# Scaled products kept in PSUM, and two small loads and scalings moved, in a windowed attention with a Sinkhorn-gated mixture of experts

## The chip, the cores and the metric

The kernel runs on one core of a Trainium2 chip: TensorE (PE; PEld is its weight load), VectorE (DVE), ScalarE (ACT), GpSimd (POOL), and SyncE (SP), which here issues all transfers. TensorE writes into PSUM, of which the kernel uses eight banks; GpSimd's operands all lie in SBUF. The metric is the time of one execution in device microseconds. The kernel before takes 1623.35 us, the median of three runs (1622.08 to 1623.9).

## What is computed

The reference, cut to what matters:

```python
scores = scale * q @ k.T, masked to 0 <= i - j < 64      # q, k, v: (4, 8, 576, 64)
x = softmax(scores) @ v                                  # as (2304, 512)
P = exp(x @ w_gate - max); 8 times: P /= rows, P /= columns, P *= N / E
for e in range(8):
    h = np.maximum(x @ w1[e], 0.0)                       # w1: (8, 512, 1024)
    out += P[:, e:e + 1] * (h @ w2[e])                   # w2: (8, 1024, 512)
```

Everything is float32. The kernel gets it from a faster matmul format by splitting each operand into a high part (rounded) and a low part (what is left), and adding three products: high x high, high x low, low x high.

## The kernel before

Attention and gate come first, up to about 200 us, together with the first half of expert 0 for all rows; for the rows of the later passes that half's output is stored in DRAM (`yd`). Then the 2304 rows go in three passes of 768 (six tiles of 128) through the remaining 7.5 experts.

The *first pass* (200 to 668 us) works in 15 units of two groups, a group being 256 hidden columns. It also prepares the weights, and stores them split in DRAM (`w1d`, `w2d`).

*Passes two and three* (668 to 1140, 1140 to 1620 us) work with blocks. A block `First` (F) makes a group of the first layer, a block `Second` (S) half of a unit's second layer. Each does a 2 x 2 block product in seven instead of eight multiplications, which are its steps 1, 5, 6, 2, 7, 3, 4, each a *product* of six matmuls with 384 columns. Its results build up in three PSUM banks: `a` gets products 1 and 2; `b` starts as a copy of `a`, gets 6, 7 and 4; `c` gets 5 and 3. In the trace they are qa, qb and qc. Each has two buffers, six banks in all, and the tag `y` takes the other two. A bank that the next product adds to must first have been read by whoever needs its present value.

In an F block (line 1005) VectorE makes from them what the second layer multiplies: relu(x) times the row's probability, in one operation (`scaled`, line 988, which reads the probabilities, spread over the partitions, from `pb`). The four results are r22 from `a` (after step 2), c22 from `b` plus a copy (step 7), cr from `c` (step 3), and sm0 from `b` (step 4); sums of these (sm0 to sm3) make slots 3 to 6 of the operand `G`, and r22, c22, cr make slots 2, 0 and 1. ScalarE writes the high part of a slot (`hi`, line 992), VectorE or GpSimd the low part (`lo`, line 996, on GpSimd for slot 2 and, in `part_s`, for the sums). The adds of an F block's step 4 (sm1, sm3 and the low part of slot 1) are put off until after step 6 of the next block (`late_sums`).

In an S block each product is added by VectorE to the output in `acc` (line 1105); the next product into that bank waits for it.

The order is written out by hand. A unit of a pass is two F blocks and the two S blocks of the unit before, in one sequence, where steps 1 and 5 of a block stand inside the block before. Each engine does its instructions in program order, and other work is hung on steps by `hook`: weight splits (ScalarE high, GpSimd low, from the buffers `wr`), loads of `w1c`, of `pb`, and between passes the new rows x (`new_x`, `high`, `low`) and the finish of the pass before: transposes (`turn`), the scaled half expert's rows (`load_y`, `scale_y`), their sum (`finish`) and the store.

## Time and profile before

| | |
|---|---|
| runs | 1623.35 us median (1622.08 to 1623.9) |
| profiled execution | 1622.74 us, of which the span is 1620.6 |
| PE busy | 1566.8 us (97%), 9665 matmuls |
| DVE busy | 1063.5 us (66%), 1745 instructions |
| ACT busy | 754.2 us (47%), 1619 |
| POOL busy | 1090.2 us (67%), 973 |
| chain that ended last | PE 69%, DVE 22%, issue 4%, ACT 2%, DMA 2% |

A row of the timeline has its start, its duration, engine, line, operation and operands, and in brackets the idle time before it with what ended that. Matmuls overlap, so the busy time of PE is no sum of work: the distance from one start to the next says what a product costs. The lines are those of the kernel before.

### The profile page before, as it was taken

What the parts mean: (1) busy time and instruction counts of PE and PEld (TensorE: products, weight loads), DVE (VectorE), ACT (ScalarE), POOL (GpSimd) and SP (SyncE); (2) the same over time, 40 slices, a digit from 0 to 9 for tenths busy, and PEclk for the clock granted to TensorE, in tenths of its full rate; (3) what the DMA queues carried; (4) which work ended last, traced back from release to release, by engine and by line L of the source; (5) the groups of instructions that cost most, each with busy time, mean ns of one, the idle gap of its engine ahead of it and who ended that gap; (6) DMA issues with size and microseconds to landing.
All of it is one profiled execution on the core that took longest, in us unless ns stands there. A gap on an engine that the chain in (4) does not pass through costs nothing.

```text
span 1620.6 us, 26692 instructions
## 1 busy us (share of the span) xinstructions
PE 1566.8 (97%) x9665; PEld 1476.6 (91%) x9665; DVE 1063.5 (66%) x1745; ACT 754.2 (47%) x1619; POOL 1090.2 (67%) x973
## 2 busy tenths in 40 slices
PE   8999999999999999899999999999799999999998
PEld 7888899899899889799999999999799999999998
DVE  7666466665455555567667667767666776676676
ACT  6666545434434434354444444445454444444443
POOL 6245476768767865277767777777777677677674
PEclk9999999999999999899999999999999999999999
DMA  9876476676767566865556555556755565565553
GB/s 222 199 174 151 126 277 235 228 253 221 269 213 258 214 224 242 286 199 198 191 172 198 190 178 187 194 185 228 245 196 175 170 211 181 167 209 184 163 188 104
DMA packets 226513, 328.32 MB, mean 203 GB/s; under 512 B 69922, under 2 KB 149390, under 8 KB 222414
## 3 DMA queue, kind: packets, MB, share of 16 engines
q1 hardware_dynamic: 226382, 326.63, 62.3%
q8 instruction: 76, 1.25, 0.3%
q14 instruction: 55, 0.45, 0.1%
HBM read 232.67 MB, written 86.96 MB: 197 GB/s over the span
## 4 chain that ended last, share of the span: by engine, by line
PE 69%; DVE 22%; issue 4%; ACT 2%; DMA 2%; POOL 0%; SPq 0%; DVEq 0%
PE yp L275 14%; PE qb L216 12%; PE qa L216 10%; PE qc L216 9%; PE qb L1097 8%; DVE sm L1003 8%; DVE G L996 4%; PE hp L561 3%; PE yp L575 3%; PE qc L1097 3%; DVE acc L1105 3%; PE qa L1097 3%; DVE sm L988 2%; DVE qc L1003 1%; DVE cr L988 1%
## 5 line engine op out<-in xcount | busy, mean ns | idle before, releaser
L216 PE MATMUL qb<-xc,w1c 128*128 128x384 f32 x1620 | 324.7, 338 | 13.6 <-DVE c L1003 7.7
L216 PEld LDWEIGHTS qb<-xc,w1c 128*128 128x128 f32 x1620 | 287.1, 189 | 15.6 <-DVE c L1003 8.4
L996 POOL TENSOR_TENSOR G<-sm,G 128x384 fp32r<-128x384 f32 x176 | 202.1, 1149 | 132.8 <-ACT G L992 132.8
L275 PE MATMUL yp<-w2c,g 128*128 128x512 f32 x1080 | 251.3, 391 | 0.5 <-DVE acc L294 0.5
L275 PEld LDWEIGHTS yp<-w2c,g 128*128 128x128 f32 x1080 | 201.7, 188 | 42.8 <-DVE acc L294 1.2
L216 PE MATMUL qa<-xc,w1c 128*128 128x384 f32 x1080 | 214.9, 338 | 0.0
L216 PE MATMUL qc<-xc,w1c 128*128 128x384 f32 x1080 | 213.0, 336 | 0.0
L216 PEld LDWEIGHTS qa<-xc,w1c 128*128 128x128 f32 x1080 | 192.3, 189 | 1.2
L216 PEld LDWEIGHTS qc<-xc,w1c 128*128 128x128 f32 x1080 | 190.1, 188 | 0.0
L1105 DVE TENSOR_TENSOR acc<-qb,acc 128x384 f32<-128x384 f32 x171 | 94.6, 553 | 122.1 <-PE qb L1097 116.5
L726 POOL TENSOR_TENSOR wp<-wr,wp 128x512 fp32r<-128x512 f32 x104 | 134.0, 1300 | 49.2 <-ACT wp L725 44.5
L177 POOL TENSOR_TENSOR w2c<-stg,w2c 128x512 fp32r<-128x512 f32 x60 | 84.5, 1429 | 108.9 <-PE qb L216 96.2
L996 POOL TENSOR_TENSOR G<-r,G 128x384 fp32r<-128x384 f32 x120 | 131.5, 1106 | 38.3 <-ACT G L992 38.2
L726 POOL TENSOR_TENSOR w2c<-wr,w2c 128x512 fp32r<-128x512 f32 x102 | 132.0, 1305 | 35.0 <-ACT w2c L725 29.1
L992 ACT CAST G<-sm 128x384 fp32r<-128x384 f32 x180 | 92.0, 511 | 99.1 <-DVE sm L1003 99.1
L1097 PE MATMUL qb<-G,w2c 128*128 128x384 f32 x552 | 114.6, 342 | 12.5 <-DVE acc L1105 12.5
L992 ACT CAST G<-r 128x384 fp32r<-128x384 f32 x120 | 61.3, 511 | 130.8 <-DVE r L988 84.0
L1097 PE MATMUL qb<-G,wp 128*128 128x384 f32 x528 | 108.8, 341 | 11.3 <-DVE acc L1105 10.7
L1097 PEld LDWEIGHTS qb<-G,w2c 128*128 128x128 f32 x552 | 96.1, 188 | 21.8 <-DVE acc L1105 21.8
L1097 PEld LDWEIGHTS qb<-G,wp 128*128 128x128 f32 x528 | 92.2, 188 | 18.9 <-DVE acc L1105 18.0
L294 DVE SCALAR_TENSOR_TENSOR acc<-yp,prob,acc 128x512 f32<-128x512 f32 x72 | 53.9, 749 | 68.5 <-PE yp L275 67.9
L457 POOL TENSOR_TENSOR s<-s,rr 128x512 f32<-128x512 f32 x36 | 37.5, 1040 | 79.3 <-DVE rr L456 71.8
(186 smaller groups left out, 2993.7 us busy)
## 6 DMA issues: line engine op xcount, KB each, us to landing
w1c<-w1d SPq DMA_DIRECT2D x120, 512.0 KB, 6.4
w1d<-w1c SPq DMA_DIRECT2D x30, 1792.0 KB, 7.5
w1c<-w1d SPq DMA_DIRECT2D x180, 256.0 KB, 3.1
stg<-in_moe_w_dram SPq DMA_DIRECT2D x66, 512.0 KB, 4.2
wr<-w2d SPq DMA_DIRECT2D x118, 256.0 KB, 3.2
wr<-in_moe_w_dram SPq DMA_DIRECT2D x88, 256.0 KB, 2.8
w2d<-tf SPq DMA_DIRECT2D x30, 512.0 KB, 4.9
pb<-prow SPq DMA_DIRECT2D x32, 192.0 KB, 7.0
```

The lines of the kernel that those rows point to most:

```text
L177: nc.gpsimd.tensor_tensor(out=w[:, 1], in0=src[:, j], in1=f32(w[:, 0]), op=ALU.subtract)
L216: nc.tensor.matmul(bank, lhsT=w[:, ws, a, kk, :], rhs=xc[xs][:, b, kk, :], start=(first and j == 0), stop=(j == 5), skip_group_check=not f ...
L275: nc.tensor.matmul(yp, lhsT=g[:, a, o:o + P], rhs=w[:, x, :], start=(i == 0), stop=(i == 11))
L294: nc.vector.scalar_tensor_tensor(out=at, in0=yp, scalar=pr, in1=at, op0=ALU.mult, op1=ALU.add)
L561: nc.tensor.matmul(hp, lhsT=w1s[c][:, a, kk, :], rhs=xs[j][:, b, kk, :], start=(i == 0), stop=(i == 3 * KD - 1))
L575: nc.tensor.matmul(yp, lhsT=g[:, a, o * P:(o + 1) * P], rhs=w[:, x, :], start=(i == 0), stop=(i == 11))
L726: nc.gpsimd.tensor_tensor(out=t[:, :, 1, :], in0=r, in1=f32(t[:, :, 0, :]), op=ALU.subtract)
L992: nc.scalar.copy(out=self.g[:, k, 0, :], in_=src)
L996: eng.tensor_tensor(out=self.g[:, k, 1, :], in0=src, in1=f32(self.g[:, k, 0, :]), op=ALU.subtract)
L1003: eng.tensor_tensor(out=dst, in0=x, in1=y, op=op)
L1097: nc.tensor.matmul(bank, lhsT=W[p, u, wp][:, g, y, cols], rhs=G7[p, 2 * u + g][:, gp, x, :], start=(start and j == 0), stop=(j == 5), skip ...
L1105: nc.vector.tensor_tensor(out=at, in0=src, in1=at, op=ALU.add)
```

## The change

The Relu'd and scaled products of an F block are written back into their banks instead of into tiles r22, c22, cr and sm0 in SBUF; c22 gets one of the two `y` banks for itself, and the transposes the other. r22, which GpSimd still reads, becomes a copy made by ScalarE. The low part of slot 2 moves to VectorE. `pb` gets one fixed buffer for even experts (`pb_a`) and one for odd ones, and the first is loaded within the first pass. The x rows for the next passes' sums take a tile of the ring `tf`. The six stored rows of the half expert are scaled in VectorE's last add (`finish`) and no longer by ScalarE; two of them have buffers of their own and are loaded earlier, and the splits of x stand a step earlier.

The diff, cut to its core:

```diff
+    pb_a = lambda: big.tile([P, 2, TP // 2, P], F32, tag="pb_a", name="pb_a")
+    PB = {}
...
-        ps["y"] = lambda: ps_m.tile([P, 512], F32, tag="y", name="yp2")
+        n_y = [0]
+
+        def y_bank(i):
+            return ps_m.tile([P, 512], F32, tag=f"y{i}", name=f"y{i}", bufs=1)
+
+        def next_y():
+            n_y[0] += 1
+            return y_bank(n_y[0] % 2)
+
+        ps["y"] = next_y
+
+        def load_pb(p, e, t):
+            PB[p, e] = t
+            rows = prow[p].rearrange("(o n e) c -> e n o c", n=2, e=E + 1)[e]
+            for n in range(2):
+                nc.sync.dma_start(out=t[:, n], in_=rows[n].partition_broadcast(P))
...
-                x = ring_b.tile([P, KD, 2 * P], F32, tag="xr2", name="xr2")
+                x = r_tf.new()
...
                 if last:
+                    load_pb(1, 0, pb_a())
                     load_w1(0)
...
-            def load_pb(p, e):
-                t = PB[p, e] = new("pb", [P, 2, TP // 2, P], F32, 2)
-                rows = prow[p].rearrange("(o n e) c -> e n o c", n=2, e=E + 1)[e]
-                for n in range(2):
-                    nc.sync.dma_start(out=t[:, n], in_=rows[n].partition_broadcast(P))
+            def next_pb(p, e):
+                load_pb(p, e, new("pb", [P, 2, TP // 2, P], F32, 1) if e % 2 else pb_a())
...
                         G.product(2, self.a, False)
-                        self.scaled(self.r22, self.a, 0)
-                        self.hi(2, self.r22)
+                        self.scaled(self.a, self.a, 0)
+                        nc.scalar.copy(out=self.r22, in_=self.a)
+                        self.hi(2, self.a)
                     elif n == 7:
-                        self.c22 = new("c22", [P, NB], F32, 1)
+                        self.c22 = y_bank(0)[:, :NB]
                         G.product(7, self.b, False)
                         self.add(self.c22, self.b, self.p5)
                         self.scaled(self.c22, self.c22, 1)
                         self.hi(0, self.c22)
-                        self.lo(2, self.r22, nc.gpsimd)
+                        self.lo(2, self.a)
                     elif n == 3:
-                        self.cr = new("cr", [P, NB], F32, 1)
                         G.product(3, self.c, False)
                         self.add(self.c, self.c, self.u2)
-                        self.scaled(self.cr, self.c, 1)
-                        self.hi(1, self.cr)
+                        self.scaled(self.c, self.c, 1)
+                        self.hi(1, self.c)
                         self.lo(0, self.c22)
...
-                        self.scaled(sm[0], self.b, 0)
-                        self.add(sm[0], sm[0], self.r22)
+                        self.scaled(self.b, self.b, 0)
+                        self.add(sm[0], self.b, self.r22)
...
                             self.add(sm[1], self.c22, sm[0], ALU.subtract)
-                            self.add(sm[3], self.cr, sm[1])
+                            self.add(sm[3], self.c, sm[1])
                             self.add(sm[2], sm[1], self.r22, ALU.add, nc.gpsimd)
-                            self.lo(1, self.cr)
+                            self.lo(1, self.c)
...
-            def load_y(p, ts):
+            def load_y(p, ts, own=False):
                 for t in ts:
-                    ys[t] = side["x"][:, ORDER[t]].rearrange("p k c -> p (k c)")[:, 0:DM]
+                    ys[t] = new("ys", [P, DM], F32, 2) if own else side["x"][:, ORDER[t - 2]].rearrange("p k c -> p (k c)")[:, 0:DM]
...
-            def scale_y(p, t):
-                nc.scalar.activation(out=ys[t], in_=ys[t], func=AF.Copy, scale=prob[:, FIRST[p] + t, 0:1])
...
-                    yps[t] = ps_m.tile([P, 512], F32, tag=bank if bank == "y" else f"q{bank}", name="yt")
+                    yps[t] = y_bank(bank) if bank in (0, 1) else ps_m.tile([P, 512], F32, tag=f"q{bank}", name="yt")
...
-                nc.vector.tensor_tensor(out=ys[t][:, cols], in0=yps[t][:, cols], in1=ys[t][:, cols], op=ALU.add)
+                nc.vector.scalar_tensor_tensor(
+                    out=ys[t][:, cols], in0=ys[t][:, cols], scalar=prob[:, FIRST[p] + t, 0:1], in1=yps[t][:, cols], op0=ALU.mult, op1=ALU.add)
...
+            next_pb(1, 1)
             out_rows(0, range(TP))
-            for e in range(2):
-                load_pb(1, e)
...
-                    for k, (blk, st) in zip(ORDER[:5], ((a, 6), (b, 5), (b, 6), (a, 7), (a, 3))):
+                    for k, (blk, st) in zip(ORDER[:5], ((a, 5), (a, 6), (b, 5), (b, 6), (a, 7))):
                         hook(blk, st, lambda k=k: (high(k), low(k, nc.gpsimd)))
-                    for k, st in zip(ORDER[5:], (7, 3)):
-                        hook(b, st, lambda k=k: high(k))
-                        hook(b, 4, lambda k=k: low(k, nc.vector))
-                    hook(b, 3, lambda p=p: load_y(p, range(3)))
-                    hook(b, 4, lambda p=p: load_y(p, range(3, 6)))
+                    for k, (blk, st) in zip(ORDER[5:], ((a, 3), (b, 7))):
+                        hook(blk, st, lambda k=k: (high(k), low(k, nc.vector)))
+                    hook(a, 2, lambda p=p: load_y(p, range(2), True))
+                    hook(b, 3, lambda p=p: load_y(p, range(2, TP)))
                     nf = plans[p][1]
-                    for t, (blk, st) in enumerate(((nf[0], 3), (nf[0], 4), (nf[1], 6), (nf[1], 2), (nf[1], 7), (nf[1], 3))):
-                        prior.setdefault((blk, st), []).append(lambda p=p, t=t: (scale_y(p, t), turn_all(p, t)))
+                    for t, (blk, st) in enumerate(((nf[0], 2), (nf[0], 3), (nf[1], 6), (nf[1], 2), (nf[1], 7), (nf[1], 3))):
+                        prior.setdefault((blk, st), []).append(lambda p=p, t=t: turn_all(p, t))
```

The rows that follow show where instructions stand on an engine, in program order: line, operation, result and operands, columns. Lines of the changed kernel are its own.

VectorE, from step 7 of a unit's second F block on into the S block, before (G_10826 is the operand, c_0_10847 is c22, L1105 are S's adds):

```order
L1003 TENSOR_TENSOR c_0_10847<-qb,p_0_10785 128x384
L988 SCALAR_TENSOR_TENSOR c_0_10847<-c_0_10847,pb_10269 128x384
L1003 TENSOR_TENSOR qc<-qc,u_0_10812 128x384
L988 SCALAR_TENSOR_TENSOR cr_10858<-qc,pb_10269 128x384
L996 TENSOR_TENSOR G_10826<-c_0_10847,G_10826 128x384
L1105 TENSOR_TENSOR acc<-qc,acc 128x384
L988 SCALAR_TENSOR_TENSOR sm_0_10885<-qb,pb_10269 128x384
L1003 TENSOR_TENSOR sm_0_10885<-sm_0_10885,r_0_10827 128x384
L1105 TENSOR_TENSOR acc<-qb,acc 128x384
L1003 TENSOR_TENSOR sm_0_10886<-c_0_10847,sm_0_10885 128x384
L1003 TENSOR_TENSOR sm_0_10887<-cr_10858,sm_0_10886 128x384
L996 TENSOR_TENSOR G_10826<-cr_10858,G_10826 128x384
```

The same place in the changed kernel (y_11164 is c22's bank, L1001 is `scaled`, L1009 `lo`, L1016 `add`, L1118 S's adds):

```order
L1016 TENSOR_TENSOR y_11164<-qb,p_0_11101 128x384
L1001 SCALAR_TENSOR_TENSOR y_11164<-y_11164,pb_a 128x384
L1009 TENSOR_TENSOR G_11142<-qa,G_11142 128x384
L1016 TENSOR_TENSOR qc<-qc,u_0_11128 128x384
L1001 SCALAR_TENSOR_TENSOR qc<-qc,pb_a 128x384
L1009 TENSOR_TENSOR G_11142<-y_11164,G_11142 128x384
L1118 TENSOR_TENSOR acc<-qc,acc 128x384
L1001 SCALAR_TENSOR_TENSOR qb<-qb,pb_a 128x384
L1016 TENSOR_TENSOR sm_0_11201<-qb,r_0_11143 128x384
L1118 TENSOR_TENSOR acc<-qb,acc 128x384
L1016 TENSOR_TENSOR sm_0_11202<-y_11164,sm_0_11201 128x384
L1016 TENSOR_TENSOR sm_0_11203<-qc,sm_0_11202 128x384
```

One row is new, the low part made from qa; the scalings have a bank as result, and the order of the others is the same.

SyncE's transfers between the first pass and the second, before (out_dram are the first pass's output rows):

```order
L949 DMA wr_7454<-w2d_148 128x512
L949 DMA wr_7456<-in_moe_w_dram 128x2x256
L949 DMA wr_7458<-w2d_148 128x512
L1158 DMA out_dram<-acc 128x512 x6
L979 DMA pb_7466<-prow_104 128x3x128 x2
L979 DMA pb_7469<-prow_104 128x3x128 x2
L949 DMA wr_7551<-in_moe_w_dram 128x2x256
```

The same place in the changed kernel; the first three rows stand at the last unit of the first pass:

```order
L723 DMA pb_a<-prow_104 128x3x128 x2
L755 DMA w1c_7248<-w1d_118 128x512 x3
L755 DMA w1c_7248<-w1d_118 128x1024 x2
...
L967 DMA wr_7457<-w2d_148 128x512
L967 DMA wr_7459<-in_moe_w_dram 128x2x256
L967 DMA wr_7461<-w2d_148 128x512
L723 DMA pb_7463<-prow_104 128x3x128 x2
L1171 DMA out_dram<-acc 128x512 x6
L967 DMA wr_7551<-in_moe_w_dram 128x2x256
```

The load of half expert 0's probabilities moves ahead by a unit's half, and that of expert 1 ahead of the output rows.

VectorE between the second pass and the third, from the fourth step of the first F block on, before (L1179 is `finish`):

```order
L988 SCALAR_TENSOR_TENSOR sm_0_12317<-qb,pb_11527 128x384
L1003 TENSOR_TENSOR sm_0_12317<-sm_0_12317,r_0_12244 128x384
L1179 TENSOR_TENSOR G_12011<-yt,G_12011 128x512
L1003 TENSOR_TENSOR sm_0_12318<-c_0_12267,sm_0_12317 128x384
L1003 TENSOR_TENSOR sm_0_12319<-cr_12278,sm_0_12318 128x384
L996 TENSOR_TENSOR G_12243<-cr_12278,G_12243 128x384
L1179 TENSOR_TENSOR G_12011<-yt,G_12011 128x512
L988 SCALAR_TENSOR_TENSOR r_1_12361<-qa,pb_11527 128x384
L1179 TENSOR_TENSOR G_12011<-yt,G_12011 128x512
L1003 TENSOR_TENSOR c_0_12378<-qb,p_0_12298 128x384
```

The same place in the changed kernel (L1189 is `finish`):

```order
L1016 TENSOR_TENSOR sm_0_12326<-y_12277,sm_0_12325 128x384
L1016 TENSOR_TENSOR sm_0_12327<-qc,sm_0_12326 128x384
L1009 TENSOR_TENSOR G_12245<-qc,G_12245 128x384
L1189 SCALAR_TENSOR_TENSOR G_12012<-G_12012,prob,y_12352 128x512
L1001 SCALAR_TENSOR_TENSOR qa<-qa,pb_a 128x384
L1189 SCALAR_TENSOR_TENSOR G_12012<-G_12012,prob,y_12370 128x512
L1016 TENSOR_TENSOR y_12377<-qb,p_0_12306 128x384
L1001 SCALAR_TENSOR_TENSOR y_12377<-y_12377,pb_a 128x384
L1009 TENSOR_TENSOR G_12359<-qa,G_12359 128x384
L1189 SCALAR_TENSOR_TENSOR G_12012<-G_12012,prob,y_12388 128x512
```

The finish is a multiply and add in one operation, and takes its first operand from the row's buffer; in the changed kernel the second row's is done before these rows, where before it stood behind the add into sm0. The bank's low part of slot 2, made from qa, stands between the last scaling of c22 and the next finish.

## Rows read from the trace of the kernel before

**Rows 1.** Stretches of the span, busy time by engine, clock, DMA

```profile
400.00:500.00 100.00, 100.00 (x507) 90.77 (x506) 52.26 (x84) 41.43 (x82) 70.97 (x66) 1.00 0.65 235
668.40:698.00 29.60, 21.20 (x103) 20.21 (x102) 14.77 (x21) 10.27 (x22) 11.86 (x9) 0.83 0.80 275
700.00:1120.00 420.00, 407.85 (x2301) 399.22 (x2300) 295.64 (x458) 194.27 (x404) 309.13 (x263) 1.00 0.58 187
1120.00:1180.00 60.00, 51.11 (x280) 48.72 (x279) 41.35 (x64) 31.01 (x61) 41.82 (x32) 0.94 0.71 240
1180.00:1600.00 420.00, 408.10 (x2302) 399.48 (x2301) 294.41 (x458) 193.78 (x403) 308.61 (x261) 1.00 0.57 184
```

**Rows 2.** Sums of waits over the span: total us, times, longest

```profile
PE qb L1097 <- DVE acc L1105: 23.2, 52, 0.7
...
ACT wp L725 <- DMA wr<-w2d: 30.9, 26, 3.2
```

**Rows 3.** One unit in order of time, TensorE

```profile
889.96 1.21 PE L1097 MATMUL qa<-G,w2c 128*128 128x384 f32 x6
...
891.46 1.32 PE L1097 MATMUL qb<-G,wp 128*128 128x384 f32 x6 [0.30 <-DVE acc L1105]
...
892.62 1.20 PE L1097 MATMUL qc<-G,wp 128*128 128x384 f32 x6
...
893.66 1.21 PE L1097 MATMUL qc<-G,w2c 128*128 128x384 f32 x6
...
895.44 1.31 PE L1097 MATMUL qb<-G,w2c 128*128 128x384 f32 x6 [0.57 <-DVE acc L1105]
...
896.58 1.20 PE L1097 MATMUL qb<-G,wp 128*128 128x384 f32 x6
```

**Rows 4.** The same stretch in order of time, VectorE

```profile
889.64 1.30 DVE L1003 TENSOR_TENSOR sm<-sm,r 128x384 f32<-128x384 f32 x1
...
890.86 0.54 DVE L1105 TENSOR_TENSOR acc<-qb,acc 128x384 f32<-128x384 f32 x1
...
894.84 0.54 DVE L1105 TENSOR_TENSOR acc<-qb,acc 128x384 f32<-128x384 f32 x1
```

**Rows 5.** Groups by shape in the stretch 700 to 1120

```profile
L996 DVE TENSOR_TENSOR G<-cr,G 128x384 fp32r<-128x384 f32 x28 | 38.5, 1375 | 0.0
...
L1003 DVE TENSOR_TENSOR sm<-c,sm 128x384 f32<-128x384 f32 x27 | 14.9, 551 | 1.5
...
L1003 DVE TENSOR_TENSOR qc<-qc,u 128x384 f32<-128x384 f32 x27 | 15.0, 555 | 0.0
...
L1015 ACT COPY p<-qc 128x384 f32<-128x384 f32 x27 | 12.9, 477 | 15.7 <-PE qc L216 15.7
```

**Rows 6.** Second boundary in order of time, VectorE, GpSimd idle

```profile
1125.34 0.56 DVE L996 TENSOR_TENSOR G<-cr,G 128x384 fp32r<-128x384 f32 x1
```

**Rows 7.** First boundary in order of time

```profile
682.43 0.56 DVE L988 SCALAR_TENSOR_TENSOR r<-qa,pb 128x384 f32<-128x384 f32 x1 [13.05 <-DMA pb<-prow]
...
683.51 4.21 PE L216 MATMUL qb<-xc,w1c 128*128 128x384 f32 x12 [6.54 <-DVE c L1003]
```

**Rows 8.** The page's costliest groups and its DMA issues

```profile
L294 DVE SCALAR_TENSOR_TENSOR acc<-yp,prob,acc 128x512 f32<-128x512 f32 x72 | 53.9, 749 | 68.5 <-PE yp L275 67.9
...
w1c<-w1d SPq DMA_DIRECT2D x180, 256.0 KB, 3.1
```

**Rows 9.** Second boundary in order of time

```profile
1145.97 1.31 PE L216 MATMUL qb<-xc,w1c 128*128 128x384 f32 x6 [1.11 <-ACT u L1020]
...
1155.38 0.66 PE L1176 MATMUL yt<-ident,acc 128*128 128x128 f32 x4 [1.52 <-DVE G L1179]
...
1155.80 1.29 PE L216 MATMUL qb<-xc,w1c 128*128 128x384 f32 x6
...
1159.94 0.69 DVE L1179 TENSOR_TENSOR G<-yt,G 128x512 f32<-128x512 f32 x1 [1.21 <-ACT G L1166]
...
1168.68 2.29 PE L216 MATMUL qb<-xc,w1c 128*128 128x384 f32 x6 [4.11 <-ACT qb L1010]
```

More of the change, by code (lines that the diff above doesn't have):

```diff
@@ L1061, in rest @@
                             self.add(sm[1], self.c22, sm[0], ALU.subtract)
[L1062 removed]
+                            self.add(sm[3], self.c, sm[1])
                             self.add(sm[2], sm[1], self.r22, ALU.add, nc.gpsimd)
[L1064 removed]
+                            self.lo(1, self.c)
                             urgent.extend([lambda k=k: self.part_s(k) for k in (1, 2, 3)])
@@ L1073, in tail @@
                         self.part_s(1, nc.vector)
-                        self.add(self.sm[3], self.cr, self.sm[1])
+                        self.add(self.sm[3], self.c, self.sm[1])
                         self.part_s(2)
@@ L1158, in out_rows, with turn @@
                     nc.sync.dma_start(out=out[(FIRST[p] + t) * P:(FIRST[p] + t + 1) * P, :], in_=acc[:, t, :])
-            def load_y(p, ts):
+            def load_y(p, ts, own=False):
                 for t in ts:
-                    ys[t] = side["x"][:, ORDER[t]].rearrange("p k c -> p (k c)")[:, 0:DM]
+                    ys[t] = new("ys", [P, DM], F32, 2) if own else side["x"][:, ORDER[t - 2]].rearrange("p k c -> p (k c)")[:, 0:DM]
                     nc.sync.dma_start(out=ys[t], in_=yd[FIRST[p] + t])
-            def scale_y(p, t):
-                nc.scalar.activation(out=ys[t], in_=ys[t], func=AF.Copy, scale=prob[:, FIRST[p] + t, 0:1])
             ys, yps = {}, {}
-            def turn(t, jh, bank="y"):
+            def turn(t, jh, bank=1):
                 o, n = divmod(t, 2)
                 if t not in yps:
-                    yps[t] = ps_m.tile([P, 512], F32, tag=bank if bank == "y" else f"q{bank}", name="yt")
+                    yps[t] = y_bank(bank) if bank in (0, 1) else ps_m.tile([P, 512], F32, tag=f"q{bank}", name="yt")
                 for h, j in jh:
@@ L1183, in window_attention_sinkhorn_moe, with turn_all @@
             ALL4 = [(h, j) for h in range(2) for j in range(2)]
-            def turn_all(p, t, bank="y"):
+            def turn_all(p, t, bank=1):
                 turn(t, ALL4, bank)
@@ L1228, in window_attention_sinkhorn_moe @@
                         if e + 1 < E:
-                            hook(F[i], 4, lambda p=p, e=e: load_pb(p, e + 1))
+                            hook(F[i], 4, lambda p=p, e=e: next_pb(p, e + 1))
                         elif more:
-                            hook(F[i], 4, lambda p=p: load_pb(p + 1, 0))
-                            hook(F[i + 3], 4, lambda p=p: load_pb(p + 1, 1))
+                            hook(F[i], 4, lambda p=p: next_pb(p + 1, 0))
+                            hook(F[i + 3], 4, lambda p=p: next_pb(p + 1, 1))
                 for u in range(n_units - 1):
@@ L1256, in last_y @@
                         side["x"] = new("G", [P, 7, 2, NB], F32, 3)
-                        load_y(p, range(TP))
+                        load_y(p, range(2), True)
+                        load_y(p, range(2, TP))
                     hook(F[n - 1], 4, last_y)
-                    for t, (blk, st) in enumerate(((a, 5), (a, 6), (b, 5), (b, 6), (a, 7), (a, 3))):
-                        hook(blk, st, lambda p=p, t=t: scale_y(p, t))
                     def before_last(p=p):
-                        for t, bank in ((1, "y"), (3, "y"), (5, "a")):
+                        for t, bank in ((1, 0), (3, 1), (5, "a")):
                             turn_all(p, t, bank)
```

2 lines of the change are left out of this document (removed).

## The prediction

> **What bounds the kernel now.** I read five views, from coarse to fine. The first is the table of stretches [rows 1]; its columns are start and end, length, then busy time and instruction count of PE, PEld, DVE, ACT and POOL, then the granted clock, the DMA share and GB/s. In each of the two long stretches some 2300 matmuls of 384 columns stand in 420 us. A product is six of them, and products that follow without a wait start 1.04 us apart (892.62 and 893.66 in [rows 3]), so a matmul costs 0.1733 us; 2301 of them are 398.8 us and 2302 are 399.0. The rest, 21.2 and 21.0 us, is time that TensorE loses in the stretches that the change rewrites. The boundary 668.4 to 698 has 103 matmuls, 17.9 us of work in 29.6: 11.7 lost, and its clock column says 0.83. The boundary 1120 to 1180 has 280, of which 24 are transposes (four take 0.42, from 1155.38 to 1155.80 in [rows 9]): 44.4 + 2.5 us of work in 60, 13.1 lost, at 0.94. The stretch 400 to 500, in the first pass, shows TensorE busy all of the time: there is nothing to win there.
>
> The second view, the sums of waits [rows 2] (total us, times, longest), names the loss: products into bank qb waited 52 times for a VectorE add at L1105, which is 13 units in each of two passes with two waits each. The third and fourth views are one unit in order of time on TensorE [rows 3] and on VectorE [rows 4]. There the product on qb starts 1.50 us after 889.96 instead of 1.04, and the following one 1.16 later: 0.58 lost. The second wait costs 1.78 - 1.04 and 1.14 - 1.04: 0.84. Together 1.42 per unit, and 26 units are 36.9 of the 42.2 us; the other 5.3 are scattered hundredths, which I leave where they are. What TensorE waits for is the add that empties qb; it stands in VectorE's queue at 890.86 and 894.84, the first behind an add of two SBUF operands that took 1.30.
>
> The fifth view, the groups by shape [rows 5] (count | busy, mean ns | idle before), shows why VectorE is late: 384 columns take 555 ns in place in PSUM, but the low part G<-cr, which reads two SBUF tensors, has a mean of 1375. That GpSimd is the cause and not the operation's own length is seen where GpSimd stands idle, at 1125.34: the same G<-cr took 0.56 [rows 6].
>
> **The change, part by part.** *In-place scaling.* The products a, b and c stay in their banks, c22 moves to a bank of its own, and all VectorE operations of a steady unit then have at most one SBUF tensor. I price each at 0.55: the in-place row (555) and an all-SBUF row that is not lengthened (551) agree [rows 5]. It frees 0.82 on each G<-cr, 0.75 on an add such as that of 889.64, and what other contended forms lose.
> *The low part of slot 2* moves from GpSimd to VectorE: one operation of 0.55 more in each group, and it must wait for ScalarE's high part, which now stands behind a new copy into r22 (0.48, the price of L1015 in [rows 5]). Behind it on VectorE are queued the add into c, its scaling, the low part of slot 0 and S's adds, for which TensorE waits.
> Does the sum fit? I lay the queue anew from the second F block's step 7. It started six products before 889.96, at 883.72, and releases VectorE 1.3 later (1.20 of duration and about 0.1), at 885.0. Then come add, scale, low 2, add, scale, low 0, S's add of step 5, scale, add: nine operations, 4.95 us, so that S's add of step 6 starts at 889.95 and ends at 890.5. TensorE wants that bank at 889.96 + 1.04 = 891.0: 0.5 to spare. Four more (subtract, add, low 1, the add from qa) and the add of step 7 ends at 893.25, where TensorE now wants the bank three products after 891.0, at 894.1. So both waits go. ScalarE needs two operations of about 0.5, the new copy and the high part, from 884.3 on, and low 2 comes at 886.1. Nothing is late next on this path; the margin is 0.5. Bounds: nothing, to all of 42.2; I take 36 of the 36.9.
>
> Bank qc is now held until low 1, some six operations or 3.3 us after step 4; the block after next wants it five products, 5.2 us, after step 4. Bank qb is wanted three products, 3.1 us, after, and its last reader is over after some 1.2. No wait.
>
> The Trainium skill has a rule that speaks against this change: "VectorE: DVE Perf Modes", section "The TRN2 errata", puts the fixed cost of a PSUM source at 120 cycles against 58 for SBUF, some 65 ns per operation (an estimate from the clock on that page). By it four of the nine operations above would grow, by 0.26 us together: the waits would still go, but the margin would halve and rival one would get a greater chance. The trace does not bear it out: the in-place row and the all-SBUF row are 4 ns apart [rows 5], so I give it no weight.
>
> *The probabilities of the half expert* are loaded in the first pass, not behind six output rows. VectorE waited 13.05 us for them and TensorE 6.54 behind it, after which twelve matmuls took 4.21 us [rows 7] where 2.08 is usual: the clock had fallen to the lower of its two levels, 1.2 GHz. With the operand there long before, steps 2 to 4 run as in any unit. Late next is the weight load for the third group: its buffer is free at step 4 of the first, its first product comes five products or 5.2 us later, and such a load takes 3.1 to land [rows 8], but output rows stand ahead of it on the queue. I leave 1.2 for that: 10.5 of 11.7 come back; bounds 6.5 (only the wait) and 11.7.
>
> *Second boundary.* The scaling of the six stored rows leaves ScalarE and becomes part of VectorE's last add, 0.75 instead of 0.69 for 512 columns (the L294 row in [rows 8], the add at 1159.94 in [rows 9]). That add's waits of 1.21 on ScalarE go, and with them the 4.11 that TensorE spent behind a copy that ScalarE reached late [rows 9]. Two low parts of x also stand earlier on VectorE. New: all transposes share one bank. From the third row on they are mostly one product apart, 1.04 + 0.42; five operations of the block before (2.75) and the third row's add (0.75) stand on VectorE when the fourth row wants the bank at 2.5 us: 1.0 lost. The sixth meets add, scale and low 2 (1.65) and the fifth's add: 1.0 lost. The ScalarE copy behind them: 0.2. The products at the start of the boundary wait for low parts, and low 2 now stands ahead of these: I leave 1.1. The 1.11 at 1145.97 behind ScalarE's queue stays, with its slow restart 1.4. That is 4.7 left of 13.1, so 8.4 come back. Bounds: 0 and 13.1.
>
> *At nothing:* the x rows in the tf ring (between their load and VectorE's reuse of the tile TensorE has a whole group, seven products or 7.3 us, in which GpSimd reads it; without that cover VectorE's sums would wait one transfer, 3.1 us for half the size [rows 8], a few times); the y banks by name; the probabilities with one buffer per parity, written, as now, when the expert two before is over. The tail pays 6 x 0.06 = 0.4 more on VectorE.
>
> **Sum** against the profiled execution, 1622.74 (span 1620.6 and 2.1 around it; the median of the runs is 1623.35, 0.6 more, which is inside their spread): 1622.7 - 36 - 10.5 - 8.4 + 0.4 = 1568.2, in round numbers 1568.
>
> **Rivals.** *One: half the unit's waits stay.* The margin of 0.5 is thin: ScalarE late by a microsecond before high 2 would bring back the first wait. For it: ScalarE stands in front of weight casts that wait for their load, 26 times 1.2 us on average [rows 2]. Against: those casts lie in the first block of a unit, the margin counts in the second. Steady gain 18 instead of 36: 1586.
> *Two: the boundaries give nothing back*, because loads that were hidden behind the waits come to light. For it: DMA share 0.80 and 275 GB/s at the first boundary, the highest of [rows 1]. Against: the queue had the same loads in the same stretch. 1622.7 - 36 + 0.4 = 1587.
> *Three: VectorE's length is not the cause* and another wait on qb takes its place at once; the boundaries alone gain: 1622.7 - 18.9 + 0.4 = 1604. Against it are [rows 3] and [rows 4], where the product starts 0.06 after the add ends.
> *Four: slower.* Low 2 holds VectorE for ScalarE. The place is the second block of a unit, the price is (hold - 0.5) in each of 26 units. With the longest cast wait of 3.2 [rows 2] it is 26 x 2.7 = 70, thus 1638. It makes the kernel slower from a hold of about 2.7 us in every unit (54.5 + 3.2 over 26, plus the margin). Against it: no such cast stands ahead of that high part.
>
> **How the numbers follow.** The forecast, 1560 to 1578, has 66 in 100; rival one 15, two 10, three 3, four 6. The low end is everything recovered, 1622.7 - 42.2 - 11.7 - 13.1 = 1555.7, so 1556; the high end takes in rivals one and two with a few us, 1592. About 0.2%, 3.2 us, is what a measurement of this kernel tells from no change. Faster than that are the first four cases, 0.94; of the last, 0.04 is slower and 0.02, the smaller holds, within.
>
> **What would show it.** In the profile after: the wait of qb for the add of S, 52 times now, gone or under ten; no VectorE row of 384 columns in the long stretches with a mean over 600 ns; those stretches with some 5 us lost instead of 21; the stretch after the first pass without a VectorE wait for pb and with a clock column near 1.00; no ScalarE scaling of the rows at the second boundary. Wrong would be: VectorE idle on ScalarE before low 2, TensorE idle on qc, in-place operations above 600 ns, or a wait for w1c in the first boundary.

## The result, and the profile after

The changed kernel takes 1567.72 us (median of 4 runs, 1567.37 to 1568.17) where the kernel before takes 1622.71 (4 runs beside it, 1621.88 to 1623.9): a ratio of 0.9661, 95% interval 0.9644 to 0.9677. The span went from 1620.6 to 1565.6 us, that is 55.0 less.

The table of stretches of the changed kernel, columns as in [rows 1]; the second line is the first boundary, the fourth the second:

```profile
400.00:500.00 100.00, 100.00 (x507) 90.87 (x506) 52.34 (x85) 41.69 (x82) 71.17 (x66) 1.00 0.66 236
668.40:690.00 21.60, 20.34 (x116) 19.70 (x115) 13.67 (x26) 12.18 (x27) 10.51 (x10) 1.00 1.04 371
700.00:1080.00 380.00, 380.00 (x2185) 380.00 (x2184) 240.18 (x463) 191.42 (x408) 244.24 (x222) 1.00 0.61 196
1080.00:1140.00 60.00, 54.97 (x317) 52.78 (x317) 39.55 (x69) 30.73 (x62) 41.51 (x33) 1.00 0.78 264
1140.00:1540.00 400.00, 400.00 (x2299) 400.00 (x2298) 250.87 (x483) 201.29 (x429) 258.57 (x234) 1.00 0.60 191
```

In the long stretches TensorE is busy all of the time: 2185 matmuls at 0.1733 us are 378.7 of 380.0. The first boundary's 116 matmuls are 20.1 of 21.6 at a clock column of 1.00, where [rows 1] had 17.9 of 29.6 at 0.83. TensorE's sums of waits (total us, times, longest) no longer hold a wait of a Second product for a VectorE add, which led [rows 2] with 23.2 us in 52 times. What is left of TensorE's waits in the rewritten stretches, longest first:

```profile
PE y L1186 <- DVE G L1189: 2.3, 2, 1.4
PE qb L218 <- ACT u L1033: 1.8, 1, 1.8
PE qb L218 <- ACT qb L1023: 1.6, 2, 1.2
...
PE qa L1110 <- DVE G L1009: 0.6, 2, 0.3
```

One unit in order of time, TensorE, which answers to [rows 3]: the products stand 1.04 us apart.

```profile
871.58 1.20 PE L1110 MATMUL qa<-G,w2c 128*128 128x384 f32 x6
872.62 1.20 PE L1110 MATMUL qb<-G,wp 128*128 128x384 f32 x6
...
875.74 1.20 PE L1110 MATMUL qb<-G,w2c 128*128 128x384 f32 x6
```

The same unit on VectorE, which answers to [rows 4]: the add that empties qb for step 7 ends at 871.86, 0.76 before its product starts (the expectations below reckon with 0.66); the next ends at 874.42, 1.32 before. In the unit's first block VectorE idles 0.73.

```profile
866.65 0.57 DVE L1016 TENSOR_TENSOR y<-qb,p 128x384 f32<-128x384 f32 x1 [0.73 <-PE qb L218]
...
871.31 0.55 DVE L1118 TENSOR_TENSOR acc<-qb,acc 128x384 f32<-128x384 f32 x1
...
873.86 0.56 DVE L1118 TENSOR_TENSOR acc<-qb,acc 128x384 f32<-128x384 f32 x1
```

Where did the 55.0 us come from? Every trace of this study has 9665 matmul records, so that the same matmul can be found in each by its number. The table gives, for stretches named by the time of before, by how many microseconds each kernel is shorter than before (first matmul to last matmul of the stretch, worked out from the starts in the two traces). The first column of numbers is the changed kernel, the others are the experiments.

```
stretch      after cr_alone gp_writes cr_back pb_early cr_pb extra1 extra3 low2_gp rows_act mended combined comb_order
668-700       10.0      1.0       1.0     9.1      7.8   8.8    7.3    4.9    10.5     10.0   10.0     10.4       10.9
700-1120      19.7     19.5      19.7     8.7      0.7  19.5   18.3  -11.8    19.7     19.7   19.7     19.5       18.9
1120-1180      6.4      1.7       2.8     3.5     -0.6   1.9    3.8    1.2     7.2      2.1    9.8     10.1       12.4
1180-1600     18.9     18.4      18.3     7.3      0.2  18.2   17.2  -15.4    19.2     18.8   17.7     19.4       18.9
to the end    -0.4      0.0       0.0    -0.4     -0.6   0.0   -0.2   -0.5    -0.4     -0.4   -0.4     -0.4       -0.4
```

Up to the first boundary the kernels differ by some 0.5 us at most.

### The profile page after: what moved, and what is told of

It reads as the page before. It is cut to its first block, busy times and chain, and to the rows that moved or that the text cites. A ratio compares the mean times of both kernels' runs of the same rounds, so it can differ in the third digit from the quotient of the medians.

```text
span 1565.6 us, 26759 instructions
## 1 busy us (share of the span) xinstructions
PE 1546.8 (99%) x9665; PEld 1473.9 (94%) x9665; DVE 970.3 (62%) x1805; ACT 764.5 (49%) x1667; POOL 979.9 (63%) x913
## 5 line engine op out<-in xcount | busy, mean ns | idle before, releaser
L1009 POOL TENSOR_TENSOR G<-sm,G 128x384 fp32r<-128x384 f32 x176 | 179.2, 1019 | 190.2 <-ACT G L1005 190.2
L277 PE MATMUL y<-w2c,g 128*128 128x512 f32 x1080 | 251.1, 391 | 0.5 <-DVE acc L296 0.5
L277 PEld LDWEIGHTS y<-w2c,g 128*128 128x128 f32 x1080 | 201.8, 188 | 42.5 <-DVE acc L296 0.9
L1118 DVE TENSOR_TENSOR acc<-qb,acc 128x384 f32<-128x384 f32 x171 | 95.0, 556 | 122.3 <-PE qb L1110 122.0
L1005 ACT CAST G<-sm 128x384 fp32r<-128x384 f32 x180 | 92.3, 513 | 65.9 <-DVE sm L1016 65.8
L1110 PE MATMUL qb<-G,w2c 128*128 128x384 f32 x552 | 111.2, 335 | 0.0
L296 DVE SCALAR_TENSOR_TENSOR acc<-y,prob,acc 128x512 f32<-128x512 f32 x72 | 53.9, 749 | 69.9 <-PE y L277 69.2
L742 ACT CAST wp<-wr 128x512 fp32r<-128x512 f32 x104 | 63.1, 620 | 63.3 <-DMA wr<-w2d 47.9
L1118 DVE TENSOR_TENSOR acc<-qc,acc 128x384 f32<-128x384 f32 x116 | 64.4, 555 | 42.2 <-PE qc L1110 42.2
L742 ACT CAST w2c<-wr 128x512 fp32r<-128x512 f32 x102 | 62.0, 621 | 57.0 <-DMA wr<-w2d 45.3
```

Source lines behind the costliest of these rows:

```text
L277: nc.tensor.matmul(yp, lhsT=g[:, a, o:o + P], rhs=w[:, x, :], start=(i == 0), stop=(i == 11))
L296: nc.vector.scalar_tensor_tensor(out=at, in0=yp, scalar=pr, in1=at, op0=ALU.mult, op1=ALU.add)
L742: nc.scalar.copy(out=t[:, :, 0, :], in_=r)
L1005: nc.scalar.copy(out=self.g[:, k, 0, :], in_=src)
L1009: eng.tensor_tensor(out=self.g[:, k, 1, :], in0=src, in1=f32(self.g[:, k, 0, :]), op=ALU.subtract)
L1110: nc.tensor.matmul(bank, lhsT=W[p, u, wp][:, g, y, cols], rhs=G7[p, 2 * u + g][:, gp, x, :], start=(start and j == 0), stop=(j == 5), skip ...
```

## Experiments

The theory: GpSimd's work beside them lengthens VectorE's operations with two SBUF operands; in the steady units this alone makes S's adds late; the boundaries have causes of their own. The main rivals: VectorE's operations with two SBUF operands are long by themselves; or the queue's length is not what TensorE waits for.

**GpSimd writes instead of reading (gp_writes).**

```
def lo(...):  if eng is nc.gpsimd: eng.memset(f32(self.g[:, k, 1, :]), 0.0); return
def add(...): if eng is nc.gpsimd: dst, x, y = dst[:, 0:48], x[:, 0:48], y[:, 0:48]
```

> The kernel before, nothing moved to PSUM, but GpSimd reads almost no SBUF in First's sums: its low parts of slots 2 to 6 write zeros instead of subtracting (they are left out of the computation), and its add of two sums covers 48 of 384 columns. GpSimd's split of the w2 parts stays. Theory (GpSimd's reading beside it lengthens VectorE's two-SBUF operations): G<-cr falls from 1375 to about 560 ns in the same place and with the same operands, the qb wait of 52 times goes, the long stretches lose under 5 us each: 1622.7 less 37 to 42, about 1583. Rival (an operation with two SBUF operands is long by itself and PSUM operands are what helps): G<-cr stays near 1375, and the time at 1622.

Measured: 1580.14 us, ratio 0.9738 (0.9722 to 0.9754). Not one operand of VectorE was moved to PSUM, and the steady stretches gained 19.7 and 18.3, within 0.6 of what the whole change gives there. The groups by shape in 700 to 1080 (busy us, mean ns) show the same G<-cr with the same SBUF operands at 645 ns instead of the 1375 of [rows 5]:

```profile
L999 DVE TENSOR_TENSOR G<-cr,G 128x384 fp32r<-128x384 f32 x26 | 16.8, 645 | 0.0
```

Two lines in order of time, GpSimd's zero writes and a VectorE operation with two SBUF operands that lies wholly within them:

```profile
1014.84 0.78 POOL L997 MEMSET G<- 128x384 f32 x2
```

```profile
1015.00 0.56 DVE L988 SCALAR_TENSOR_TENSOR c<-c,pb 128x384 f32<-128x384 f32 x1
```

It took 0.56, and so did all six of these in 700 to 1080 that had only zero writes beside them (557 to 559 ns): GpSimd's writing does not lengthen it, its reading does. The Trainium skill says this in "SBUF — State Buffer", section "Who interferes with whom": a VectorE instruction with two SBUF inputs contends with a GpSimd instruction that reads SBUF, not with one that only writes it. These lines agree. What is left on G<-cr, 645 instead of some 550 ns, stands on all 26 of them (642 to 647); beside each lie the end of GpSimd's 48-column add and zero writes, and which of the two costs it is not shown.

**Only cr in place (cr_alone), on the kernel before.**

```
-    self.cr = new("cr", [P, NB], F32, 1)
+    self.cr = self.c
```

> The kernel before with one of its edits: cr is the bank qc itself (scaled in place); c22, sm0, the low part of slot 2, the probabilities and the second boundary stay as they were. Theory (a VectorE operation that reads two SBUF operands is lengthened by GpSimd's work beside it, and what matters is where such operations stand in the queue): the two operations on cr fall from 1.2 to 1.4 us to 0.55 in both blocks of a unit, the add of S's step 7 is in time, and the first wait of a unit shrinks from 0.58 to about 0.2, because the add of two SBUF operands (1.30 at 889.64 before) still stands ahead of S's step 6. Loss per unit 0.2 instead of 1.42, 26 units: about 32 us, thus 1591. Rival (the four edits share the gain evenly): a quarter of 41 us, 1612. Rival (VectorE's length is not the cause): 1622.

Measured: 1582.47, ratio 0.9755 (0.974 to 0.9769), 8.5 us better than the theory's 1591. One line gave 19.5 and 18.4 in the steady stretches, all but 0.7 of what the whole change gives there. My forecast had left the add at 889.64 at 1.30 [rows 4]. On VectorE, in order of time, that add is short now and another operation, which has more room behind it, is the long one:

```profile
877.92 1.28 DVE L996 TENSOR_TENSOR G<-c,G 128x384 fp32r<-128x384 f32 x1
...
880.17 0.56 DVE L1003 TENSOR_TENSOR sm<-sm,r 128x384 f32<-128x384 f32 x1
880.65 0.55 DVE L1105 TENSOR_TENSOR acc<-qb,acc 128x384 f32<-128x384 f32 x1
```

The add of step 6 ends at 881.20 and its product starts, on time, at 881.76. With the chain through cr shorter, VectorE and GpSimd meet at other places: the operations that contend are set by when the two queues meet, not by their kind alone. In 700 to 1080 half of the 26 G<-c began while GpSimd was at such an operation and took 952 to 1286 ns, half had none beside them and took 546 to 549; the mean is 902, and it costs TensorE nothing.

**Only cr undone (cr_back), on the changed kernel.**

```
-    self.scaled(self.c, self.c, 1)
+    self.cr = new("cr", [P, NB], F32, 1)
+    self.scaled(self.cr, self.c, 1)
     ...                                     # and what read self.c reads self.cr
```

> The changed kernel with one edit undone: cr is an SBUF tile again (the scaling reads qc and writes cr, the sum and the low part of slot 1 read cr). Theory: the two operations on cr are again 1.2 to 1.4 us where GpSimd works beside them, 1.5 us more per block; the first block's excess is taken up by the 0.73 us that VectorE idles and the margin of about 0.66 before S's step 6, the second block's by the margin of 1.3 before step 7, so that some 0.3 per unit comes back: about 1576 (1570 to 1590). Rival (cr was the whole of the steady gain): 1567.7 + 37 to 41 = 1605 to 1609. Rival (VectorE's length does not matter now): 1568.

Measured: 1593.51, ratio 0.9821 (0.9806 to 0.9835): 25.8 slower than the changed kernel, between the theory's 8 and the rival's 37 to 41, and outside the theory's range. VectorE in order of time:

```profile
869.36 1.29 DVE L1016 TENSOR_TENSOR sm<-cr,sm 128x384 f32<-128x384 f32 x1
870.57 1.37 DVE L1009 TENSOR_TENSOR G<-cr,G 128x384 fp32r<-128x384 f32 x1
...
872.33 0.55 DVE L1016 TENSOR_TENSOR y<-qb,p 128x384 f32<-128x384 f32 x1
...
877.00 0.55 DVE L1119 TENSOR_TENSOR acc<-qb,acc 128x384 f32<-128x384 f32 x1
...
879.07 1.36 DVE L1009 TENSOR_TENSOR G<-cr,G 128x384 fp32r<-128x384 f32 x1
...
880.82 0.54 DVE L1119 TENSOR_TENSOR acc<-qb,acc 128x384 f32<-128x384 f32 x1
```

and TensorE:

```profile
881.42 1.33 PE L1111 MATMUL qb<-G,w2c 128*128 128x384 f32 x6 [0.42 <-DVE acc L1119]
```

The first block's 1.5 eats the idle 0.73 (no idle before 872.33 now) and the rest is carried on: step 6's add is just in time, and step 7's meets the rest and the second block's 1.3. I had set each excess against its own margin; lateness on an in-order engine adds up until the engine idles. The two gains aren't shares of a sum either: cr alone gives 37.9 in the steady stretches, everything but cr 16.0, both together 38.6.

**VectorE's margin (extra1, extra3), on the changed kernel.** With k = 1 and k = 3:

```
-    self.lo(0, self.c22)
+    for _ in range(k + 1):
+        self.lo(0, self.c22)
```

> The changed kernel with one VectorE operation more in every First block: the low part of slot 0 is computed twice in a row (same result), 0.47 us more in the queue ahead of S's adds. Theory (TensorE waits only when the adds of S come after their product's start; the trace of after has VectorE idle 0.73 in the first block of a unit and 0.66 to spare before S's step 6): the first block's 0.47 goes into the idle time, the second's into the margin, and the time stays at 1567.7, within 3. Rival (each VectorE operation on this path costs its length): 26 x 0.47 to 52 x 0.47 us, 1580 to 1592.

Measured: 1574.68, ratio 0.9705 (0.9691 to 0.972), 7.0 slower than the changed kernel, outside the theory's 3. A steady unit is as it said: the idle time of the first block has shrunk from 0.73 to 0.19, the add starts at 876.04, and the product at 876.75 is on time.

```profile
870.78 0.57 DVE L1016 TENSOR_TENSOR y<-qb,p 128x384 f32<-128x384 f32 x1 [0.19 <-PE qb L218]
...
876.04 0.55 DVE L1119 TENSOR_TENSOR acc<-qb,acc 128x384 f32<-128x384 f32 x1
```

By the table (from the profiled executions, whose spans are 8.7 apart) 5.3 of the loss stand at the two boundaries, 2.7 and 2.6, and 3.1 in the two long stretches together, where two single products wait (0.6 and 1.2 us). So the rival's 26 or 52 times 0.47 is not what is lost; but the boundaries have no such margin, and I had not counted them.

> The same with the low part of slot 0 computed four times: 1.41 us more in every First block. Theory: of the first block's 1.41 the idle time takes 0.73 and 0.68 is carried on; with the second block's 1.41 S's step 6 add is 2.09 later against a margin of 0.66, and TensorE loses 1.4 in each of 26 units: 1567.7 + 37 = 1605 (1595 to 1612). Rival (lateness isn't carried from block to block): 26 x 0.75 = 20, 1587. Rival (VectorE's length is not the cause): 1568.

Measured: 1643.53, ratio 1.0129 (1.0114 to 1.0144): slower than before, and 38 us beyond the theory. TensorE has two waits in each unit, not one (sums of waits):

```profile
PE qb L1111 <- DVE acc L1119: 24.2, 26, 1.1
PE qb L218 <- ACT u L1033: 24.0, 27, 1.8
```

The first is the one forecast. The second is ScalarE's, in order of time, with TensorE behind it:

```profile
914.71 0.51 ACT L1005 CAST G<-sm 128x384 fp32r<-128x384 f32 x1 [2.51 <-DVE sm L1016]
915.13 0.47 ACT L1033 COPY u<-qb 128x384 f32<-128x384 f32 x1
```

```profile
915.65 1.34 PE L218 MATMUL qb<-xc,w1c 128*128 128x384 f32 x6 [0.85 <-ACT u L1033]
```

The copy of u needs nothing from VectorE, but it is queued on ScalarE behind a cast that does. So VectorE's lateness reaches TensorE by a second way. That delay in VectorE's queue costs TensorE time holds, but the theory knew one way for it and there are two. Of the 75.8 us that extra3 loses against the changed kernel, 65.8 stand in the long stretches, and its two sums of waits are about equal. Rival four of the prediction was built on the first way alone: for 2 x 1.41 = 2.8 us a unit its price, (hold - 0.5) x 26, is 60.

**The low part of slot 2 (low2_gp), on the changed kernel.**

```
-    self.lo(2, self.a)
+    self.lo(2, self.r22, nc.gpsimd)
```

> The changed kernel with one edit undone: the low part of slot 2 is again GpSimd's, from the copy r22. VectorE has one operation less in each First block, GpSimd one of 1.02 us more. Theory (VectorE is no longer waited for, GpSimd has room, and that low part has no other work to be late for): the time stays, 1567.7 within 3. Rival (that low part holds VectorE for ScalarE's high part in the changed kernel, rival four of the prediction in small): faster by 5 or more. Rival (GpSimd's low parts of slots 3 to 6 come late for Second's products): slower by 5 or more.

Measured: 1566.25 (1565.65 to 1566.74), ratio 0.9654 (0.9638 to 0.967). Against the changed kernel that is 1.5 less, inside the theory's 3 (the intervals of the two ratios overlap): the steady stretches are the same within 0.3, and 0.5 and 0.8 came at the two boundaries. Moving this operation to VectorE bought nothing that the runs show; GpSimd has room for it, and there it lengthens nothing, since no VectorE operation of a steady unit has two SBUF operands any more.

**The probabilities alone (pb_early), on the kernel before.** The edit is the change's own: load_pb(1, 0, pb_a()) in the first pass, next_pb(1, 1) ahead of out_rows, and the x rows in the tf ring.

> The kernel before with one part of the change: the first expert's probabilities are loaded in the first pass into a tile of their own, the second's ahead of the six output rows (and x for the sums in the tf ring, which makes the room). Theory: VectorE's wait of 13.05 us for pb goes, the stretch after the first pass loses about 2 us instead of 11.7 at a clock near 1.00, and all else stays: 1622.7 - 9.5 = 1613. Rival (other loads come to light there): the stretch loses as much as before, 1622.

Measured: 1614.82, ratio 0.9951 (0.9937 to 0.9966): 7.9 less, of the 9.5 expected. Its first boundary and its steady wait:

```profile
668.40:690.00 21.60, 19.72 (x103) 19.08 (x102) 14.84 (x22) 10.56 (x22) 12.59 (x10) 0.92 0.99 343
```

```profile
PE qb L1101 <- DVE acc L1109: 22.7, 52, 0.6
```

103 matmuls in 21.6 instead of the changed kernel's 116. With pb there in time, the contended operations stand on the path of this boundary too: from 679.08 on, three VectorE operations with two SBUF operands take 1.47, 1.26 and 1.35, the add into c comes behind them at 683.52, and TensorE waits 1.8 for it.

**Both (cr_pb), on the kernel before**: the edits of cr_alone and pb_early.

> The kernel before with two edits: cr is the bank qc itself, and the first expert's probabilities are loaded in the first pass. Theory (the two stand in different stretches and add up; alone they gave 40.2 and 7.9, and the in-place cr helps the first boundary by 1 to 2 more once the long wait there is gone): 1622.6 - 40.2 - 7.9 - 1 to 2 = 1573 (1572 to 1575), which leaves about 5 of the whole change for c22, sm0, the low part of slot 2 and the second boundary's edits together. Rival (each had hidden what the other uncovers): 1578 or more.

Measured: 1573.84, ratio 0.9699 (0.9685 to 0.9713), in the theory's 1572 to 1575. Two of the change's edits give 48.9 of its 55.0. What is missing is 1.2 at the first boundary and 4.5 at the second, where the old wait, the longer of these two, is still there:

```profile
PE qb L218 <- ACT qb L1014: 5.3, 2, 4.1
```

**The finishing rows scaled by ScalarE (rows_act), on the changed kernel.**

```
+    if p == 1:
+        nc.scalar.activation(out=ys[t], in_=ys[t], func=AF.Copy, scale=prob[:, FIRST[p] + t, 0:1])
+        nc.vector.tensor_tensor(out=ys[t][:, cols], in0=yps[t][:, cols], in1=ys[t][:, cols], op=ALU.add)
+        ...                                  # the store, as in the other branch
```

> The changed kernel with one edit undone at the second boundary: the six stored rows are scaled by ScalarE (512 columns, one operation each) ahead of VectorE's finishing add, at the new places and with the new banks; the tail keeps the fused add. Theory (the prediction's second boundary: the fused scaling takes the finishing adds and the copies behind them out of ScalarE's queue): of the 6.4 us that the second boundary gained, 3 to 5 are lost again, 1571 to 1573. Rival (the boundary's gain came from shorter VectorE operations and earlier low parts, ScalarE has room): 1567.7 within 1.

Measured: 1572.16, ratio 0.969 (0.9674 to 0.9705): 4.4 lost again, 4.3 of it at the second boundary. VectorE's sums of waits in 1080 to 1150 name it:

```profile
DVE ys L1191 <- ACT ys L1190: 4.9, 2, 4.2
DVE G L1191 <- ACT G L1190: 3.2, 4, 1.5
```

Without the fused scaling two thirds of that boundary's 6.4 are gone.

**What was left at the second boundary (mended), on the changed kernel.**

```
-  ... (nf[1], 2), (nf[1], 7), (nf[1], 3)         all in bank 1
+  ... (nf[1], 2) in bank 0, (nf[1], 7), (nf[1], 4)
+  if self.i or self.p == 1:                      # First.step(5)
       do_bulk(1)
```

> The changed kernel with three edits at the second boundary only: the fourth row's transposes go to bank 0 instead of 1, the sixth row's stand after step 4 of the second First block instead of after step 3, and the next pass's first step 5 takes no w2 part from the queue, so that the copy of u does not stand behind a cast that waits for its load. Theory: the waits of 1.39 and 0.89 for VectorE's finishing add of the row before and the one of 1.80 for ScalarE's copy of u go, with their restarts 1.56 + 1.06 + 1.97 = 4.6; something small comes to light: 1563.5 (1562 to 1566). Rival (the same time is lost a little later, as the weight parts come later): 1567.7.

The restart counted there adds 0.17 to each wait; part of it is that the product behind one that waited starts 1.14 to 1.16 later instead of 1.04.

Measured: 1564.97, ratio 0.9645 (0.9631 to 0.966), 2.8 less than the changed kernel. The boundary gained 3.4, and the next stretch lost 1.2, at three places (0.4, 0.6 and 0.2 near 1165, 1333 and 1459) far behind the boundary. The rival, that the time is lost again a little later, does not follow from that: the next run has the same three edits and loses nothing there (19.4 in the table).

**All that helped (combined), and step 1 one place earlier (combined_order).** The first has the edits of mended and low2_gp; the second also this:

```
-  (6, 2, 7, 3, 4, -1, -5) if k == 1
+  (6, 2, 7, 3, -1, 4, -5) if k == 1
```

> The changed kernel with the three edits at the second boundary of the run called mended and GpSimd's low part of slot 2 of the run called low2_gp. Theory (they gave 2.8 and 1.5 in different queues): 1563.5 (1562.5 to 1565). Rival (mended's gain was partly the same microseconds at the start of that boundary): 1565.

> The same, and in the second First block of each pass step 1 of the next block stands before step 4, not behind it, so that its ScalarE copy is not queued behind casts that wait for VectorE's step 4. Theory: the wait of 1.17 for that copy at the first boundary (with its restart 1.4) and the like one of 0.8 at the second go; the load of w1c, which this product needs, has 4.2 us instead of 5.2 and landed in 3.1: 1563.5 - 2.4 = 1561. Rival (w1c's load comes late there): 1563.5 or more.

Measured: 1563.42 (0.9635, 0.9621 to 0.9649) and 1561.93 (0.9626, 0.9613 to 0.964). The last beats both kernels: its interval lies below the changed kernel's. Its second boundary, in the columns of [rows 1]:

```profile
1080.00:1140.00 60.00, 59.81 (x351) 58.92 (x350) 42.77 (x74) 33.65 (x69) 48.14 (x40) 1.00 0.83 281
```

It holds 351 matmuls where the changed kernel has 317 in as long a stretch; of the 13.1 us that before lost there, 12.4 are back. Of the 2.4 forecast for the move of step 1, 1.5 came; the runs of combined alone spread over 3.4 (1561.98 to 1565.35), so its size is uncertain.

## Why the prediction was right, and where it was not

The forecast was 1568 and the time 1567.72. The parts:

- **Steady units: 36 forecast, 38.6 measured** (19.7 + 18.9). The mechanism is shown from two sides: gp_writes takes GpSimd's reading away and leaves VectorE's operands, cr_alone takes an SBUF operand away and leaves GpSimd. The 36.9 of both waits went, and 1.7 of the 5.3 scattered hundredths that I had left.
- **In-place operations at 0.55: right.** By shape in 700 to 1080 of the changed kernel, with GpSimd's add beside them, which answers to [rows 5]:

```profile
L1016 DVE TENSOR_TENSOR sm<-qc,sm 128x384 f32<-128x384 f32 x26 | 14.5, 558 | 3.1
...
L1009 DVE TENSOR_TENSOR G<-qc,G 128x384 fp32r<-128x384 f32 x26 | 14.2, 547 | 0.0
```

- **The rule against it** (the Trainium skill, "VectorE: DVE Perf Modes", section "The TRN2 errata", a dearer PSUM source) does not show: 547 and 558 from PSUM against 551 all-SBUF [rows 5].
- **The margin of 0.5 before S's step 6**: it is 0.76 from the end of the add to the start of the product, and the later one, put at 0.85, is 1.32. extra1 shows that in a steady unit half a microsecond is there, and extra3 that 1.41 per block is not. What the step left out is the second way, over ScalarE's casts; rival one spoke of ScalarE being late, but not of VectorE making it so.
- **The low part of slot 2 "one operation of 0.55 more"**: in the steady units nothing, as forecast; at the boundaries 1.3 (low2_gp). In the steady units VectorE had no idle time before it (0.0 on 26 in 700 to 1080).
- **First boundary: 10.5 forecast, 10.0 measured.** The size is right; what fills the rest is not what I said, in this trace: I left 1.2 for w1c's load, and TensorE waited for none. It waited for ScalarE, whose copy stands behind a cast that waits for VectorE (in order of time):

```profile
685.62 0.51 ACT L1005 CAST G<-sm 128x384 fp32r<-128x384 f32 x1 [0.28 <-DVE sm L1016]
...
686.04 0.47 ACT L1023 COPY qb<-qa 128x384 f32<-128x384 f32 x1
...
686.56 1.34 PE L218 MATMUL qb<-xc,w1c 128*128 128x384 f32 x6 [1.17 <-ACT qb L1023]
```

  But the load is close behind. The kernel of mended is the same up to there and gains the same 10.0, and in its trace it is the product for the third group that waits, for w1c, as forecast:

```profile
684.68 1.33 PE L218 MATMUL qa<-xc,w1c 128*128 128x384 f32 x6 [0.96 <-DMA w1c<-w1d]
```

  And "steps 2 to 4 run as in any unit" needed the in-place operations: pb alone gave 7.8. The clock column is 1.00, as forecast.
- **Second boundary: 8.4 forecast, 6.4 measured**, the worst term. I left 4.7; about 6.7 stayed. The ScalarE queue that I put at 1.4 cost 2.06 (the product is due 1.04 after 1114.30), behind a weight cast that waits for its load:

```profile
1114.30 1.30 PE L218 MATMUL qa<-xc,w1c 128*128 128x384 f32 x6
...
1116.35 0.62 ACT L742 CAST wp<-wr 128x512 fp32r<-128x512 f32 x1 [2.50 <-DMA wr<-in_moe_w_dram]
...
1116.88 0.47 ACT L1033 COPY u<-qb 128x384 f32<-128x384 f32 x1
...
1117.40 1.31 PE L218 MATMUL qb<-xc,w1c 128*128 128x384 f32 x6 [1.80 <-ACT u L1033]
```

  The transposes that share one bank, put at 1.0 each, came 1.65 and 1.14 late (due 1.04 after 1123.53 and 1128.19):

```profile
1123.53 1.30 PE L218 MATMUL qa<-xc,w1c 128*128 128x384 f32 x6
1126.22 0.66 PE L1186 MATMUL y<-ident,acc 128*128 128x128 f32 x4 [1.39 <-DVE G L1189]
...
1128.19 1.29 PE L218 MATMUL qc<-xc,w1c 128*128 128x384 f32 x6
1130.37 0.66 PE L1186 MATMUL y<-ident,acc 128*128 128x128 f32 x4 [0.89 <-DVE G L1189]
```

  So ScalarE's queue was put 0.7 too low and the two transposes together 0.8; the copy behind them, put at 0.2, came 0.6 late (at 1134.62, due 1.04 after 1132.96). The places were right, the sizes optimistic. For the fourth row I had the five operations and the third row's add in 3.5 and the bank wanted at 2.5; VectorE began them at 1122.54, behind the second row's add, and was through 3.6 later, but the row was due at 1124.57, only 2.0 later. That the fused scaling gives the larger part of the gain here is shown (rows_act).
- **Tail: 0.4 forecast, 0.4 measured.**

So that the sum fits to 0.3 is luck: errors cancel, 2.6 too little in the units and 2.5 too much at the boundaries. The mechanism is as forecast. Rivals one and two were refuted by the stretches, rival three by gp_writes and extra3. Rival four is not what happened; extra3 shows that a hold of that size does make the kernel slower, at a higher price than rival four had.

Open: mended's three edits were not tried one by one, and why its trace loses 1.2 in the stretch behind the boundary, where combined loses nothing, is not shown.

## What to carry to other kernels

When a wait is for an in-order engine that is not full, look for the few operations that are longer than others of their shape, and for what ran beside them: here one tile moved from SBUF to PSUM gave seven tenths of the gain, 40 of 55 us. Count lateness along the whole queue until the engine idles, and follow it over every engine whose own queue has a waiting instruction ahead of something that TensorE needs. And after a large wait is gone, the boundaries between stages are where the next microseconds lie: here other banks, places or engines for two rows' transposes, a weight cast, a low part and a product gave 5.8 us more.

## What the runs showed of the hardware

The lengthening goes both ways, and it falls on the one that starts second. Before, in order of time, beside the 889.64 of [rows 4], which took 1.30:

```profile
889.52 1.01 POOL L996 TENSOR_TENSOR G<-sm,G 128x384 fp32r<-128x384 f32 x1
```

```profile
891.33 0.54 DVE L1003 TENSOR_TENSOR sm<-c,sm 128x384 f32<-128x384 f32 x1
```

```profile
891.56 1.18 POOL L996 TENSOR_TENSOR G<-sm,G 128x384 fp32r<-128x384 f32 x1 [1.04 <-ACT G L992]
```

At 889.52 GpSimd is first and keeps its 1.01, and VectorE has the loss; at 891.33 VectorE is first and keeps its 0.54, and GpSimd has it. The trace of before has no exception in 700 to 1120, where operations that overlap by less than 0.06 us count as alone. Of VectorE's 162 operations of 384 columns with two SBUF operands, the 54 alone took 548 to 561 ns, the 13 that began before GpSimd's 542 to 543, and the 95 that began while one of GpSimd's was running 606 to 1368. GpSimd's own of 384 columns took 1003 to 1025 alone or first (84) and 1182 to 1341 second (82).

By means, GpSimd's add r<-sm,r had 1328 ns in 700 to 1120 before; where VectorE's partner operation has a PSUM operand it is 1018 (cr_alone), and with only cr undone 1336 (cr_back):

```profile
L1003 POOL TENSOR_TENSOR r<-sm,r 128x384 f32<-128x384 f32 x26 | 26.5, 1018 | 0.0
```

```profile
L1016 POOL TENSOR_TENSOR r<-sm,r 128x384 f32<-128x384 f32 x24 | 32.1, 1336 | 0.0
```

So coming second costs a VectorE operation of this size up to 0.8 and one of GpSimd's up to 0.3, and the edit that frees the one frees the other: GpSimd's busy time fell from 1090.2 to 979.9 us in the changed kernel, more than the 60 operations of 1.1 us (66 us) that moved to VectorE.
